# Routed attention and a gated FFN on one core: where the fill pieces of a unit begin, and a few one-hots, casts and copies put elsewhere

## The chip, the cores and the metric

The kernel runs on one core of a Trainium2 chip. A core has TensorE (matmuls, called PE in the profile), VectorE (DVE), ScalarE (ACT), GpSimd (POOL) and SyncE (SP), which work side by side, each through its own list of instructions in order, and wait for each other by semaphores. The metric is the device time of the program in microseconds, as the median of several executions. The profile is of one execution, and its span runs from the first to the last instruction, so it is a little shorter than the metric.

## The reference

First attention for 4 batches of 8 heads, 768 tokens and a head size of 64. Each query and each key is assigned to one of 16 clusters of its head, and a query sees only the keys of its own cluster. Then RMS norm and a gated FFN over 3072 tokens.

```python
q_assign = argmax(q_n @ c_n)          # 16 centroids for each head
k_assign = argmax(k_n @ c_n)
mask = q_assign[:, :, :, None] == k_assign[:, :, None, :]
scores = where(mask, scale * q @ k.T, -1e9)
attn = softmax(scores)
x = (attn @ v) as [3072, 512]
xn = x / sqrt(mean(x * x) + 1e-6) * rms_g
out = (silu(xn @ w_gate) * (xn @ w_val)) @ w_out      # 512 -> 1536 -> 512
```

## The kernel before

The work is cut into 8 units: four batches, two halves of the queries each. A unit has 8 heads, and a head 3 steps, each of which makes the scores of two blocks of 128 keys against 384 queries and one exponential. What PE does between two such steps is called a gap, so a unit has 24 gaps. The mask is in the matmul itself: below the 64 rows of a head's keys and queries lie 16 rows of one-hots of the cluster, so that an equal cluster adds a large number, which the bias of the exponential takes away again.

In PSUM there are two score tiles, one accumulator for a pair of heads (the pair is divided out of it before the next pair may use it), and three general tiles, which transposes, cluster products, gates, values and outputs share.

```python
ps_s = pool("ps_s", 2, space=PSUM)
ps_a = pool("ps_a", 1, space=PSUM)
ps_g = pool("ps_g", 3, space=PSUM)
```

A head goes through these helpers. `trans` turns tokens so that the head size lies on partitions, and has ACT or DVE copy the result out of PSUM. `cast` makes bf16 keys or queries of it (two halves each: K0, K1, Q0, Q1). `pair_clusters` finds the cluster of every token of two heads on PE and DVE. `under`, called by `head`, puts the one-hots below keys and queries with DVE transposes. `vcast` makes bf16 values on GpSimd. `pv` multiplies with the values and, at every second head, divides.

```python
def trans(g, h, part, on=None):
    ...                                     # 3 PE transposes into a ps_g tile
    if on is nc.vector:
        nc.vector.tensor_scalar_mul(to, ps, by)
    else:
        nc.scalar.activation(to, ps, ACT.Copy, scale=by)

def head(n):
    under(n, 1)                             # one DVE transpose for the keys
    under(n, 0)                             # and one for the queries

def pv(u, h):
    ...
    if h % 2 == 0:
        accs[u] = ps_a.tile([P, 2, HT, D + 1], F32, tag="acc", name="acc")
    ...                                     # 18 matmuls pT x vbf
    if h % 2:
        nc.vector.reciprocal(inv[:, :, :nt], acc[:, :, :nt, D])
        nc.vector.tensor_tensor(dst, acc[:, :, :nt, :D], ..., op=ALU.mult)
```

In unit 0 what goes into each gap is written out by hand. Gaps not named get `more`, one filler matmul on constants that keeps PE busy; gaps with `None` get nothing.

```python
early = [lambda h=h, m=m: trans(1, h, m, nc.vector if h > 2 else None) for h in (2, 3) for m in (1, 0)]
first = {0: lambda: trans(1, 0, 0), 1: gap1, 2: early[0], 3: early[1], 4: lambda: (early[2](), early[3]()), 5: gap5,
         6: None, 7: lambda: (head(4), head(5)), 9: lambda: pair_clusters(3), 10: None,
         13: lambda: (head(6), head(7)), 14: lambda: (more(), second_batch())}
```

From unit 1 on the gaps are filled with pieces of the FFN of the units before and with the preparation of heads to come. Each piece has a cost, and the rule spreads them evenly over the gaps. In units 2 to 7 the pieces are, in order: the last 8 gate and value products of unit u-2, the RMS norm of unit u-1, the output products of unit u-2 and the transposes of unit u-1, and then the gates and values of unit u-1 with the transposes, casts and clusters of the heads to come.

```python
def attention(heads, fill, skip=0, hooks={}):
    gaps = [(u, h, i) for u, h in heads for i in range(UNITS[u][2])]
    total, done, n = sum(c for c, _ in fill), 0.0, 0
    for at, (u, h, i) in enumerate(gaps):
        scores(u, h, i)
        if i == (0 if (u, h) == (1, 0) else 1):
            for p in due:
                pv(*p)                      # the head before this one
            due[:] = [(u, h)]
        ...
        while n < len(fill) and at >= skip and done <= total * (at + 1 - skip) / (len(gaps) - skip):
            done += fill[n][0]
            fill[n][1]()
            n += 1
```

Of the kernel before, what the change touches and what calls it, by code (L numbers as in the profile page):

```python
# [22 lines left out]
def kernel(  # L23
# [12 lines left out]
    nc = tc.nc  # L36
    B, H, S, D = q.shape
# [8 lines left out]
    NG = B * H // HG  # L46
    UNITS = [(b, c, HT) for b in range(B) for c in (0, HT)]
    NU = len(UNITS)
    CC = DM // P
# [4 lines left out]
    CUT = CC + 2 * FC - 8  # L54
# [30 lines left out]
    def load_qk(n):  # L85
        if n < B * H:
            load(n, 0)
            load(n, 1)
# [102 lines left out]
    def load_gv(i):  # L191
        c = slice(i * DF // 4, (i + 1) * DF // 4)
        for w, of in ((wg, moe_w_gate), (wv, moe_w_val)):
            nc.gpsimd.dma_start(out=w[:, :, c], in_=of[:, c].rearrange("(c p) f -> p c f", p=P))
# [7 lines left out]
    def trans(g, h, part, on=None):  # L202
        if (g, h // 2) not in qkT:
            qkT[g, h // 2] = qk32.tile([P, 2, 2, UQ], F32, tag="qkT", name="qkT")
        qk = staged[g * HG + h]
        ps = ps_g.tile([P, UQ], F32, tag="gen", name="tq")
        for i in range(HT):
            nc.tensor.transpose(ps[:, i * P:(i + 1) * P], qk[:, part, 2 * i:2 * i + 2].rearrange("p t d -> p (t d)"),  # L208
                                ident_f)
        to, by = qkT[g, h // 2][:, h % 2, part], 1.0 / ZS if part else 1.0  # L210
# [4 lines that stand above are left out]
# [5 lines left out]
    def cast(on, g, h, part, es=(0, 1)):  # L220
        for e in es:
            to = cols((kext if part else qext)[g % 4][:D, h], g, e)
            of = qkT[g, h // 2][e * D:(e + 1) * D, h % 2, part]
            if on is nc.scalar:
                nc.scalar.copy(to, of)
            else:
                on.tensor_copy(to, of)  # L227

    def vcast(n):
        nc.gpsimd.tensor_copy(vbf[n // HG % 4][:, n % HG, :, :D], stagedv[n])  # L230
# [62 lines left out]
    def slot(n, m):  # L293

        return 32 * (2 * (n % 2) + m if n < 2 else 2 * m + n % 2)

    def pair_clusters(p, heads=(0, 1)):
        g, h = divmod(2 * p, HG)
        what = [(h + i, m) for i in heads for m in range(2)]
        at = [slot(2 * p + i, m) for i in heads for m in range(2)]  # L300
        r = slice(min(at), max(at) + 32)
        pool = ps_g if p else ps_s
        ps = pool.tile([P, UQ], F32, tag="gen" if p else "s", name="sc")
        for a, (hh, m) in sorted(zip(at, what)):
            nc.tensor.matmul(ps[a:a + 32], lhsT=cblk[:, g * HG + hh], rhs=qkT[g, hh // 2][:, hh % 2, m],
                             start=True, stop=True)
        sct = asg.tile([P, UQ], F32, tag="scT", name="scT", bufs=2)
        nc.vector.transpose(sct[r], ps[r])
        cl = sct[r].rearrange("p (b e c) -> p b e c", e=2, c=NC)
        mx = small.tile([P, NB, 2], F32, tag="mx", name="mx")[r]  # L310
        nc.vector.tensor_reduce(mx, cl, axis=AX, op=ALU.max)
        nc.vector.tensor_tensor(pads[p][r, :, :NC].rearrange("p b c e -> p b e c"), cl,
                                mx.unsqueeze(3).broadcast_to([mx.shape[0], NB, 2, NC]), op=ALU.is_equal)

    def under(n, m):
        i = slot(n, m)
        nc.vector.transpose((kext if m else qext)[n // HG][D:D + 32, n % HG].bitcast(I32),
                            pads[n // 2][i:i + 32].rearrange("p b c e -> p (b c e)").bitcast(I32))
# [181 lines left out]
    def weave(t, c):  # L500

        return [x for pair in zip(t, c) for x in pair] + c[len(t):]

    def group(g):
        t, c, a = group_work(g)
        return [x for h in range(HG) for x in t[2 * h:2 * h + 2] + c[2 * h:2 * h + 2]] + a

    def spread(a, b):

        if not a:  # L510
            return list(b)
        w, n = [], 0
        for i, x in enumerate(a):
            w.append(x)
            while n < len(b) * (i + 1) // len(a):
                w.append(b[n])
                n += 1
        return w
# [12 lines left out]
    def border(o, ffn):  # L531

        return o[:-2] + ffn[:2] + o[-2:-1] + ffn[2:4] + o[-1:]
# [6 lines left out]
    def head(n):  # L540
        under(n, 1)
        under(n, 0)

    def casts(on, n, *what):
        for m, e in what:
            cast(on, n // HG, n % HG, m, (e,))

    K0, K1, Q0, Q1 = (1, 0), (1, 1), (0, 0), (0, 1)
    pool_ = nc.gpsimd
# [32 lines left out]
    def more():  # L582
        busy(1, False)
# [3 lines left out]
    def second_batch():  # L587
        nc.sync.dma_start(out=hold, in_=invs[0].rearrange("p a t -> p (a t)"))
        for n in range(H + HG, H + NQ):
            load_qk(n)  # L590
        for n in range(H, H + NV):
            load_v(n)
# [13 lines left out]

    def gap5():
        pair_clusters(2)
        casts(pool_, 6, Q0, K0, K1)
        vcast(4)  # L610
        casts(pool_, 7, Q0)
        for n in (4, 5):
            casts(pool_, n, Q1)
        vcast(5)
        casts(pool_, 7, K0, K1)
        vcast(6)
        load_gv(2)
        vcast(7)
        for n in (6, 7):
            casts(pool_, n, Q1)  # L620
        load_gv(3)

    early = [lambda h=h, m=m: trans(1, h, m, nc.vector if h > 2 else None) for h in (2, 3) for m in (1, 0)]
    late = [lambda h=h, m=m: trans(2, h, m, nc.vector if h < 3 else None) for h in range(HG) for m in (1, 0)]
    first = {0: lambda: trans(1, 0, 0), 1: gap1, 2: early[0], 3: early[1], 4: lambda: (early[2](), early[3]()), 5: gap5,
             6: None, 7: lambda: (head(4), head(5)), 9: lambda: pair_clusters(3), 10: None,
             13: lambda: (head(6), head(7)), 14: lambda: (more(), second_batch())}
    first.update({16: None, 19: None, 22: None})
    first.update({i: f for i, f in zip((15, 17, 18, 20, 21, 23), late)})

# [3 lines left out]
# [7 lines that stand above are left out]
                    pv(*p)  # L641
                due[:] = [(u, h)]
            if h == H - 1:
                squares(u, i, False)
            if (u, h, i) in hooks:
                hooks[u, h, i]()
# [4 lines that stand above are left out]
        for _, f in fill[n:]:  # L651
            f()

    attention([(0, h) for h in range(H)], [], hooks={(0, *divmod(i, HT)): f for i in range(H * HT) for f in [first.get(i, more)] if f})
    for u in range(1, NU):
        ffn, o, g = ffn_work(u - 1), out_work(u - 2) if u > 1 else [], u + 2
        if u == 1:
            t, c, a = group_work(2)
            t3, c3, a3 = group_work(3)
            n = LEAD - 4  # L660
            o3 = [(0.0, lambda i=i: load_o(i)) for i in range(0, FC, 4)]
            w = weave(t3[n:], c3)
            prep = c + a + w[:6] + spread(w[6:], o3) + a3[:5]
            idle = const.tile([P, 1], BF16)

            def norm():
                rms(0)
                nc.gpsimd.tensor_copy(idle, xn[0][:, HT - 1, DM - 1:])
                for h in range(HG):
                    casts(pool_, H + h, K0, Q0, K1, Q1)  # L670

            hooks = {(1, 0, 0): late[6], (1, 0, 1): lambda: (late[7](), norm())}
            hooks.update({(1, *divmod(2 + i, HT)): t3[i][1] for i in range(n)})
            hooks[1, *divmod(LEAD - 1, HT)] = lambda: xtrans_all(0)
            fill = spread(ffn[CC:CUT], prep)
            attention([(1, h) for h in range(H)], fill, LEAD, hooks)
        else:
            fill = ffn_work(u - 2)[CUT:] + [(0.0, lambda u=u: rms(u - 1))]
            fill += border(spread(o[:3], [(0.0, f) for _, f in a3[5:]]) + o[3:], ffn) if u == 2 else border(o, ffn)
            attention([(u, h) for h in range(H)], fill + spread(ffn[CC:CUT], group(g) if g < NG else []), 1)  # L680
    rest = ffn_work(NU - 2)[CUT:]
    rest[0][1]()
    pv(NU - 1, H - 1)
# [38 lines left out]
```

## Time and profile before

| what | value |
|---|---|
| time, median of 3 | 346.6 us (346.44 to 346.74) |
| span of the profiled execution | 344.7 us |
| PE busy | 337.5 us (98%) |
| ACT busy | 259.0 us (75%) |
| DVE busy | 222.5 us (65%) |
| POOL busy | 113.2 us (33%) |
| TensorE clock granted | 1.000 |

How to read it: "busy" counts the time in which at least one instruction of the engine runs. Rows of the timeline give the start in us, the length in us of a run of like instructions, engine, line of the kernel and operation, what is written and read, and how many. Square brackets at the end give the idle time of the engine just before, and what ended it. L333 are score matmuls and L337 their exponentials, L351 the products with the values, L358 the divisions, L423 gates and values, L448 the output products, L208 transposes, L212 and L214 their copies by DVE and ACT, L227 casts, L230 casts of values, L317 one-hots, L305 and L241 cluster products, L376 the squares of the norm, and L117 filler.

### The profile page before, as it was taken

What the parts mean: (1) busy time and instruction counts of PE and PEld (TensorE: products, weight loads), DVE (VectorE), ACT (ScalarE), POOL (GpSimd) and SP (SyncE); (2) the same over time, 40 slices, a digit from 0 to 9 for tenths busy, and PEclk for the clock granted to TensorE, in tenths of its full rate; (3) what the DMA queues carried; (4) which work ended last, traced back from release to release, by engine and by line L of the source; (5) the groups of instructions that cost most, each with busy time, mean ns of one, the idle gap of its engine ahead of it and who ended that gap; (6) DMA issues with size and microseconds to landing.
All of it is one profiled execution on the core that took longest, in us unless ns stands there. A gap on an engine that the chain in (4) does not pass through costs nothing.

```text
span 344.7 us, 7997 instructions
## 1 busy us (share of the span) xinstructions
PE 337.5 (98%) x3044; PEld 208.4 (60%) x3044; DVE 222.5 (65%) x540; ACT 259.0 (75%) x447; POOL 113.2 (33%) x227
## 2 busy tenths in 40 slices
PE   8999999999999999999999999999999999999996
PEld 4546657555765567565675656755566656655654
DVE  6999797976578626785367745686356645675330
ACT  5889979856888768886797777888778877764322
POOL 6999696234336205180132702435000000000000
PEclk9999999999999999999999999999999999999999
DMA  7999979982450014400130010000100001001002
GB/s 269 360 226 210 240 170 231 159 271 89 143 164 17 27 62 152 139 22 35 61 94 2 23 62 32 2 8 18 63 32 0 2 33 61 2 1 64 30 2 91
DMA packets 27302, 31.62 MB, mean 92 GB/s; under 512 B 4480, under 2 KB 24320, under 8 KB 27264
## 3 DMA queue, kind: packets, MB, share of 16 engines
q1 hardware_dynamic: 18608, 25.02, 22.3%
q0 software_dynamic: 8368, 5.71, 10.3%
q8 instruction: 24, 0.39, 0.5%
q10 hardware_dynamic: 288, 0.39, 0.3%
q14 instruction: 14, 0.11, 0.1%
HBM read 28.35 MB, written 6.29 MB: 100 GB/s over the span
## 4 chain that ended last, share of the span: by engine, by line
PE 87%; ACT 5%; POOL 3%; DVE 2%; DMA 1%; issue 1%; ACTq 0%; POOLq 0%; DVEq 0%
PE gate L423 17%; PE o L448 17%; PE val L423 17%; PE s L333 16%; PE acc L351 9%; PE tq L208 4%; ACT pT L337 4%; PE sc L241 3%; PE tx L396 1%; POOL kext L227 1%; DMA qk<-in_q_dram 1%; PE warm L117 1%; POOL qext L227 1%; PE o L459 1%; ACT xn L376 1%
## 5 line engine op out<-in xcount | busy, mean ns | idle before, releaser
L337 ACT ACTIVATE pT<-s,off 128x768 bf16<-128x768 f32 x192 | 170.8, 904 | 34.7 <-PE s L333 33.6
L333 PE MATMUL s<-qext,kext 80*128 80x384 bf16 x384 | 94.2, 327 | 1.6 <-ACT pT L337 0.6
L432 DVE SCALAR_TENSOR_TENSOR th<-th,gate 128x384 f32<-128x384 f32 x84 | 46.4, 552 | 50.3 <-ACT th L431 50.1
L423 PE MATMUL gate<-xnT,wg 128*128 128x384 bf16 x384 | 78.5, 325 | 0.1
L423 PE MATMUL val<-xnT,wv 128*128 128x384 bf16 x384 | 78.1, 326 | 0.0
L448 PE MATMUL o<-wo,gvT 128*128 128x512 bf16 x276 | 67.6, 379 | 0.0
L227 POOL CAST qext<-qkT 64x384 bf16<-64x384 f32 x64 | 34.5, 546 | 75.0 <-ACT qkT L214 66.6
L333 PEld LDWEIGHTS <-kext 80*128 80x128 bf16 x384 | 36.6, 98 | 31.2 <-issue 7.5
L431 ACT ACTIVATE th<-gate 128x384 f32<-128x384 f32 x84 | 41.2, 491 | 13.9 <-PE gate L423 13.5
L423 PEld LDWEIGHTS <-wv 128*128 128x128 bf16 x384 | 36.1, 97 | 25.3 <-issue 3.4
L423 PEld LDWEIGHTS <-wg 128*128 128x128 bf16 x384 | 35.9, 97 | 24.6 <-issue 3.3
L436 DVE SCALAR_TENSOR_TENSOR gvT<-th,val 128x384 bf16<-128x384 f32 x84 | 46.2, 549 | 6.1 <-PE val L423 1.4
L351 PEld LDWEIGHTS <-pT 128*128 128x128 bf16 x1152 | 43.5, 97 | 10.6 <-DVE x L358 1.3
L351 PE MATMUL acc<-vbf,pT 128*128 128x65 bf16 x1152 | 45.7, 193 | 1.2 <-POOL vbf L230 0.7
L448 PEld LDWEIGHTS <-gvT 128*128 128x128 bf16 x276 | 25.7, 97 | 25.5 <-issue 0.6
L208 PE MATMUL tq<-ident_f,qk 128*128 128x128 f32 x192 | 30.7, 279 | 0.0
L282 POOL DMA_DIRECT2D qext<-oh x40 | 19.1, 486 | 30.2 <-DVE oh L271 24.2
L397 DVE TENSOR_SCALAR xnT<-tx,gcol 128x384 bf16<-128x384 bf16 x28 | 10.6, 413 | 28.5 <-PE tx L396 28.5
L214 ACT ACTIVATE qkT<-tq 128x384 f32<-128x384 f32 x55 | 26.0, 494 | 3.6 <-PE tq L208 3.2
L208 PEld LDWEIGHTS tq<-ident_f,qk 128*128 128x128 f32 x192 | 23.8, 143 | 6.6 <-ACT qkT L214 1.0
L451 ACT COPY o_sb<-o 128x512 f32<-128x512 f32 x23 | 13.5, 586 | 17.7 <-PE o L448 17.7
L282 POOL DMA_DIRECT2D kext<-oh x40 | 19.1, 485 | 10.1 <-DVE oh L271 10.1
(81 smaller groups left out, 250.3 us busy)
## 6 DMA issues: line engine op xcount, KB each, us to landing
qk<-in_q_dram SPq DMA_DIRECT2D x32, 192.0 KB, 4.3
vs<-in_v_dram SPq DMA_DIRECT2D x32, 192.0 KB, 4.3
out_dram<-o_sb SPq DMA_DIRECT2D x23, 256.0 KB, 2.0
qk<-in_k_dram SPq DMA_DIRECT2D x30, 192.0 KB, 4.3
wg<-in_moe_w_gate_dram POOLq DMA_DIRECT2D x4, 384.0 KB, 8.1
wv<-in_moe_w_val_dram POOLq DMA_DIRECT2D x4, 384.0 KB, 10.5
wo<-in_moe_w_out_dram POOLq DMA_DIRECT2D x3, 512.0 KB, 8.8
qext<-oh POOLq DMA_DIRECT2D x40, 12.0 KB, 1.6
```

Of the source, the lines that this page charges most:

```text
L208: nc.tensor.transpose(ps[:, i * P:(i + 1) * P], qk[:, part, 2 * i:2 * i + 2].rearrange("p t d -> p (t d)"), ident_f)
L214: nc.scalar.activation(to, ps, ACT.Copy, scale=by)
L227: on.tensor_copy(to, of)
L282: on.dma_start(out=ext[D:D + NC, h, e * UQ:(e + 1) * UQ], in_=put[g, m][32 * h + e * NC:32 * h + (e + 1) * NC])
L333: nc.tensor.matmul(ps[:, j, :w] if nt == HT else flat[:, j * w:(j + 1) * w], lhsT=cols(kext[g % 4][:KR, hh], g, kc // HT, kc % HT * P, (kc ...
L337: nc.scalar.activation(pT[u, h][:, n * i:n * i + n, :w], of, ACT.Exp, bias=off, scale=scale * ZS)
L351: nc.tensor.matmul(acc[:, h % 2, t], lhsT=pT[u, h][:, kc, t * P:(t + 1) * P], rhs=vbf[g % 4][:, hh, kc % HT * 2 + kc // HT], start=kc == 0 ...
L423: nc.tensor.matmul(ps, lhsT=w[:, c, f * P:(f + 1) * P], rhs=xnT[u][:, c, :n], start=c == 0, stop=c == CC - 1)
L431: nc.scalar.activation(th, ps, ACT.Tanh, scale=0.5)
L432: nc.vector.scalar_tensor_tensor(th, th, 1.0, ps, op0=ALU.add, op1=ALU.mult)
L436: nc.vector.scalar_tensor_tensor(gvT[u][:, f, :n], gates[u], 0.5, ps, op0=ALU.mult, op1=ALU.mult)
L448: nc.tensor.matmul(outs[u], lhsT=gvT[u][:, f, t * P:(t + 1) * P], rhs=wo[:, f], start=f == 0, stop=f == FC - 1)
```

## The change

Its title is that a unit's pieces begin at its first gap instead of its second: `attention` gets no `skip` of 1 any more in units 2 to 7, so that pieces are placed from gap 0 on, and spread over 24 gaps rather than 23. It does so from a kernel that lacks some of what the one before has, so these go back at the same time:

- head 7's transposes are copied out of PSUM by ACT instead of DVE;
- head 6's keys are cast by DVE in gap 13 instead of by GpSimd in gap 5;
- the one-hots of head 4 are made in gap 5 instead of gap 7, and those of head 6 in gap 10 instead of gap 13, which puts them ahead of the divisions on DVE's list;
- gap 6 of unit 0 gets a filler matmul;
- the three loads of output weights are spread over all of the preparation of unit 1 but its first part, instead of starting six pieces later.

```diff
     def gap5():
         pair_clusters(2)
-        casts(pool_, 6, Q0, K0, K1)
+        casts(pool_, 6, Q0)
         vcast(4)
 ...
         load_gv(3)
+        head(4)
 
-    early = [lambda h=h, m=m: trans(1, h, m, nc.vector if h > 2 else None) for h in (2, 3) for m in (1, 0)]
+    early = [lambda h=h, m=m: trans(1, h, m) for h in (2, 3) for m in (1, 0)]
 ...
-             6: None, 7: lambda: (head(4), head(5)), 9: lambda: pair_clusters(3), 10: None,
-             13: lambda: (head(6), head(7)), 14: lambda: (more(), second_batch())}
+             7: lambda: head(5), 9: lambda: pair_clusters(3), 10: lambda: head(6),
+             13: lambda: (casts(nc.vector, 6, K0, K1), head(7)), 14: lambda: (more(), second_batch())}
 ...
-            w = weave(t3[n:], c3)
-            prep = c + a + w[:6] + spread(w[6:], o3) + a3[:5]
+            prep = c + a + spread(weave(t3[n:], c3), o3) + a3[:5]
 ...
-            attention([(u, h) for h in range(H)], fill + spread(ffn[CC:CUT], group(g) if g < NG else []), 1)
+            attention([(u, h) for h in range(H)], fill + spread(ffn[CC:CUT], group(g) if g < NG else []))
```

## Prediction

> **What bounds the kernel now.** I read the page first (busy time, then the chain that ended last), then a table of busy time by stage, then the instructions of TensorE and ScalarE in order of time in two places: the first unit (11 to 36 us) and the six places where one unit follows another. The page:
>
> ```profile
> PE 337.5 (98%) x3044; PEld 208.4 (60%) x3044; DVE 222.5 (65%) x540; ACT 259.0 (75%) x447; POOL 113.2 (33%) x227
> PE 87%; ACT 5%; POOL 3%; DVE 2%; DMA 1%; issue 1%; ACTq 0%; POOLq 0%; DVEq 0%
> ```
>
> TensorE (PE) is busy for 98% of the span, and 87% of the chain of waits is its work. The 98% is flattered, since the ends of matmuls are modelled and overlap the next start; so I count from start to start. In units 1 to 7 the stage table leaves it no idle time that could be seen:
>
> ```profile
> 41.00:107.36 66.36, 66.35 (x632) 40.98 (x631) 49.25 (x119) 52.61 (x85) 31.87 (x64) 1.00 0.66 168
> 107.36:148.40 41.04, 41.04 (x379) 25.69 (x377) 26.17 (x65) 32.78 (x60) 13.68 (x29) 1.00 0.26 83
> 267.40:304.20 36.80, 36.60 (x338) 22.74 (x338) 20.48 (x49) 29.67 (x53) 0.00 (x0) 1.00 0.06 23
> ```
>
> The columns are stretch, length, then busy time and count of PE, weight loads, DVE, ACT and POOL, then clock, DMA share and GB/s. Unit 3 (107.36 to 148.40) has 41.04 us of PE in 41.04, and ACT only 32.78. So from 41 us on the kernel is bound by TensorE, and only lost TensorE time can be won. Before that, in unit 0, ACT sets the pace. Its exponentials run in unbroken rows, and what stands in brackets is the little it waits:
>
> ```profile
> 16.30 1.72 ACT L337 ACTIVATE pT<-s,off 128x768 bf16<-128x768 f32 x2
> 18.35 3.28 ACT L337 ACTIVATE pT<-s,off 128x768 bf16<-128x768 f32 x4 [0.33 <-PE s L333]
> 21.86 0.90 ACT L337 ACTIVATE pT<-s,off 128x768 bf16<-128x768 f32 x1 [0.24 <-PE s L333]
> 23.10 4.92 ACT L337 ACTIVATE pT<-s,off 128x768 bf16<-128x768 f32 x6 [0.34 <-PE s L333]
> 28.70 1.69 ACT L337 ACTIVATE pT<-s,off 128x768 bf16<-128x768 f32 x2 [0.68 <-PE s L333]
> ```
>
> Six exponentials take 4.92 us in a row, 0.82 each. (A gap is one third of a head: two score matmuls and one exponential. Head h has gaps 3h to 3h+2.)
>
> **What the Trainium skill says.** "Perfetto Trace Analysis", section "Tensor Engine Instruction (MATMUL, LD_WEIGHTS)", says that the profiled end of a matmul is estimated, not observed, and that ACT, DVE and GpSimd take their work strictly in order. The trace agrees on the first: a gate piece of four matmuls is shown 0.81 us long, and the next begins 0.65 us after it. The second is what makes the order of emission in unit 0 matter; the DVE records of this trace stand in the order of the program. The same page, section "Identifying the Most-Contended Engine", warns that matmul busy time says little about closeness to the roofline; I use it only to find who waits. "ScalarE: Activation LUTs", section "What ACT_TABLE_LOAD costs", says that back-to-back activations overlap by about 93 ns; here one exponential is 904 ns on the page and 820 in a row, which agrees. "GPSIMD Engine Reference", section "Elementwise — side-by-side cycle accounting", has VectorE about twice as fast elementwise; here a 64x384 cast has a median of 504 ns on POOL and of 354 on DVE, so a factor of 1.4.
>
> **Part 1: pieces from the first gap (the title of the change).** With skip 1, the first gap of units 2 to 7 holds only its two score matmuls, so two pairs of scores follow each other at once, and then the product of the previous unit's last head. Two matmuls of a pair start 0.33 us apart from the next work (265.87 to 266.20), so four need 0.65. The trace at the borders from unit 1 to 2, from 2 to 3, and from 6 to 7:
>
> ```profile
> 65.33 0.98 PE L333 MATMUL s<-qext,kext 80*128 80x384 bf16 x4
> 66.16 0.53 PE L351 MATMUL acc<-vbf,pT 128*128 128x65 bf16 x12
> ```
>
> ```profile
> 107.36 0.89 PE L333 MATMUL s<-qext,kext 80*128 80x384 bf16 x4
> 108.08 0.28 PE L351 MATMUL acc<-vbf,pT 128*128 128x65 bf16 x4
> ```
>
> ```profile
> 266.85 0.49 PE L333 MATMUL s<-qext,kext 80*128 80x384 bf16 x2
> 267.60 0.48 PE L333 MATMUL s<-qext,kext 80*128 80x384 bf16 x2 [0.27 <-ACT pT L337]
> 267.93 0.71 PE L351 MATMUL acc<-vbf,pT 128*128 128x65 bf16 x18
> ```
>
> From the first score to the product it is 0.83, 0.72 and 1.08 us where 0.65 would do: 0.18, 0.07 and 0.43 lost. The second pair needs the score buffer of the last exponential of the old unit (there are two buffers), and that is not done; from unit 6 to 7 it is worst because ACT also makes squares there. The borders 3 to 4, 4 to 5 and 5 to 6 look like 2 to 3 (148.39 to 149.12, 189.44 to 190.16, 230.48 to 231.20): 0.07 each. Sum: 0.18 + 4 x 0.07 + 0.43 = 0.89 us.
>
> Working the fill rule through by hand (a piece is placed while the cost placed so far is no more than the share of the gaps passed), skip 0 puts two pieces, a gate and a value product, into gap 0 of every unit from 2 on. They are 1.3 us of PE between the two pairs of scores, more than the 0.43. So the waits go. In the last gaps of a unit the rule places the same pieces as before, so the load on ACT there stays. The RMS norm still comes behind the product of head 7 (gap 4 instead of 5), and the transposes that need it about five gaps later. No piece is added. This part: **-0.9 us**, less whatever of the wait reappears; I count -0.75.
>
> **Part 2: head 7's two copies go from DVE to ACT (gap 4, unit 0).** DVE loses the two at 18.23, 1.02 us together. ACT gains two, about 0.40 each in a row (three took 1.26 us at 9.40): 0.8 us between the exponentials of gaps 4 and 5. ACT stood idle for 0.33 before gap 6, and its exponential of gap 5 ended at 18.02, so gap 6 starts at about 18.02 + 0.8 - 0.1 = 18.7 rather than 18.35. **+0.3 us**, carried by the full score buffers to gap 10 (22.2 instead of 21.86).
>
> **Part 3: one-hots of heads 4 and 6 ahead of the divisions.** One-hots are two DVE transposes, 2 x 0.60 us. DVE without the two copies reaches the clusters of the third pair at 18.2 instead of 19.17, ends them at about 20.2, then makes head 4's one-hots (1.2) and only then the division, which ends at about 22.15 instead of 21.95. These are the rows before:
>
> ```profile
> 21.39 0.56 DVE L358 TENSOR_TENSOR x<-acc,inv 128x384 f32<-128x384 f32 x1
> 22.00 0.72 PE L351 MATMUL acc<-vbf,pT 128*128 128x65 bf16 x18 [0.18 <-DVE x L358]
> 26.66 0.56 DVE L358 TENSOR_TENSOR x<-acc,inv 128x384 f32<-128x384 f32 x1
> 27.61 0.71 PE L351 MATMUL acc<-vbf,pT 128*128 128x65 bf16 x18 [0.68 <-POOL vbf L230]
> ```
>
> The division frees the only accumulator. So head 2's product starts at 22.2 instead of 22.0, and gap 11's exponential at about 23.3 instead of 23.1: the 0.3 of part 2 becomes 0.2, not 0.5, because both waits stand side by side. The second division ends at about 27.4 instead of 27.2.
>
> **Part 4: head 6's key casts go from POOL to DVE.** POOL loses two casts in a row (1.44 us at 25.55), so the value cast at 27.05 comes at about 25.6. That cast is what head 4's product waited for until 27.61. Now the accumulator, free at about 27.4, is the last wait: gap 17's exponential at about 28.55 instead of 28.70. The casts cost DVE some 0.4 us each behind that division, so head 7's one-hots end near 29.4 (29.6 before). From 28.70 on ACT runs without a break to the end of the unit. Parts 2 to 4 together: **-0.15 us**.
>
> **Part 5: the rest.** One more filler matmul in gap 6, 0.2 us of PE that ACT hides. Head 5 and later heads still get their one-hots before their scores. The output weights are loaded earlier and spread wider in unit 1; PE shows no wait for them, so 0.
>
> Sum: 346.6 - 0.75 - 0.15 = **345.7 us**.
>
> **Rivals.** (a) ACT's extra 0.8 us stays on the path: unit 0 would end 0.3 to 0.8 us later, and with part 1 the time would be 346.2 to 346.7. For it: ACT is full from 28.70. Against it: the 0.68 us wait ahead of that absorbs it. (b) The waits at the borders only move: ACT does the same work, and a unit whose gaps hold less PE work (1.15 instead of 1.20 of the rule's cost in units with head preparation, 0.99 instead of 1.04 in unit 7) leaves it less time. Against it: the page has ACT 75% busy, and no other score in units 2 to 7 waits 0.2 us or more for it. The time would be 346.3. (c) Other phasing of pieces with the three general PSUM buffers: in unit 3 the value piece beside the cluster products starts 0.15 late (106.71, where 106.56 would do). If that shifts by 0.1 per unit, it is +-0.5 in all. (d) DVE becomes the bound of unit 0 (10.70 us busy of the 11.20 from 18.8 to 30): if the strided casts cost 0.7 each, head 7's one-hots slip to about 30, still ahead of its scores at 31.24. No loss.
>
> **Range and chances.** Part 1 lies between 0 and -0.9, parts 2 to 4 between -0.4 and +0.6, phasing adds +-0.4. That gives 345.0 to 346.6 at 8 in 10, with 345.7 in the middle. Two per cent are 6.9 us; nothing in the sum comes near it.
>
> **What would show it.** Right: at each border the two pairs of scores stand 1.0 us or more apart with gate and value pieces between, and the row waiting 0.27 us for ACT is gone; the PE idle of 267.4 to 304.2 drops; unit lengths from 107 to 230 go from 41.04 to just under 41.0. In unit 0, ACT's idle before gap 6 is gone, head 4's product waits for a division instead of a cast, and the row of exponentials that began at 28.70 begins at 28.4 to 28.7. Wrong, if unit 0 ends later than 28.70 + 8 exponentials (35.2) by more than 0.5 us, or if new PE waits appear within units 2 to 7.

## The result and the profile after

The changed kernel takes **348.28 us** (median of 4, 347.92 to 348.38), the kernel before 346.67 beside it: a ratio of 1.0046, 95% interval 1.0028 to 1.0063. It is 1.6 us slower where 0.9 us less was forecast. The page of the changed kernel, its busy times and its chain:

```profile
PE 338.8 (98%) x3045; PEld 208.4 (60%) x3045; DVE 221.3 (64%) x540; ACT 261.1 (75%) x449; POOL 112.8 (33%) x225
PE 85%; DVE 8%; ACT 5%; issue 1%; POOL 0%; ACTq 0%; DVEq 0%; POOLq 0%
```

The busy times hardly differ. The chain does: DVE holds 8% of it where it held 2%, and GpSimd, with 3% before, is gone. A share of the chain is not a loss, and part of this one lies in unit 0 (the page's list of the chain by line has L312 and L317 there with 1% each). But L432 and L436, which empty gates and values, and the key casts of L227 are in it too, with 1% each. That points to places where PE waits for DVE, which a page with PE busy for 98% in both kernels doesn't show.

The first question is whether the two gains that were forecast came at all. ScalarE in unit 0, in order of time:

```profile
17.94 4.12 ACT L337 ACTIVATE pT<-s,off 128x768 bf16<-128x768 f32 x5
22.28 0.90 ACT L337 ACTIVATE pT<-s,off 128x768 bf16<-128x768 f32 x1 [0.22 <-PE s L333]
23.46 4.91 ACT L337 ACTIVATE pT<-s,off 128x768 bf16<-128x768 f32 x6 [0.28 <-PE s L333]
28.55 6.45 ACT L337 ACTIVATE pT<-s,off 128x768 bf16<-128x768 f32 x8 [0.17 <-PE s L333]
```

The idle 0.33 us ahead of gap 6 is gone, filled by the two copies. Gap 10 comes at 22.28 instead of 21.86, and gap 17 at 28.55 instead of 28.70, its wait down from 0.68 to 0.17. Unit 0 is as forecast.

The border from unit 2 to unit 3, TensorE in order of time:

```profile
107.83 0.49 PE L333 MATMUL s<-qext,kext 80*128 80x384 bf16 x2
108.15 0.81 PE L423 MATMUL gate<-xnT,wg 128*128 128x384 bf16 x4
108.80 0.81 PE L423 MATMUL val<-xnT,wv 128*128 128x384 bf16 x4
109.45 0.49 PE L333 MATMUL s<-qext,kext 80*128 80x384 bf16 x2
109.78 0.40 PE L351 MATMUL acc<-vbf,pT 128*128 128x65 bf16 x8
```

Each piece starts when the one before has done: 0.32, 0.65, 0.65, 0.33. Nothing waits. From unit 6 to 7 it is the same (scores at 269.08 and 270.71, product at 271.04, a gate and a value between). So the gain at the borders came too, less 0.12 us that a value behind the first border now loses (70.07, due at 69.95).

The loss lies inside units 2 to 5. A unit, from one cluster product to the same in the next unit, takes 41.65 us (184.50 to 226.15) where it took 41.04 (182.81 to 223.85).

In unit 3 two places stand out where a matmul starts later than the ones before it need. TensorE and DVE there, all engines in order of time, some rows left out:

```profile
131.44 0.81 PE L423 MATMUL val<-xnT,wv 128*128 128x384 bf16 x4
...
132.41 0.90 PE L208 MATMUL tq<-ident_f,qk 128*128 128x128 f32 x6
132.74 0.35 DVE L227 CAST kext<-qkT 64x384 bf16<-64x384 f32 x1
133.13 0.55 DVE L436 SCALAR_TENSOR_TENSOR gvT<-th,val 128x384 bf16<-128x384 f32 x1
133.15 0.49 PE L333 MATMUL s<-qext,kext 80*128 80x384 bf16 x2
...
133.74 0.81 PE L423 MATMUL gate<-xnT,wg 128*128 128x384 bf16 x4
...
138.23 0.81 PE L423 MATMUL gate<-xnT,wg 128*128 128x384 bf16 x4
...
139.21 0.82 PE L208 MATMUL tq<-ident_f,qk 128*128 128x128 f32 x6
...
139.65 0.55 DVE L432 SCALAR_TENSOR_TENSOR th<-th,gate 128x384 f32<-128x384 f32 x1
140.25 0.81 PE L423 MATMUL val<-xnT,wv 128*128 128x384 bf16 x4 [0.23 <-DVE th L432]
```

Scores from 133.15 are done at 133.48, but the gate starts at 133.74: 0.26 lost. Two transposes from 139.21 need 0.65, but the value starts at 140.25: 0.39 lost. In both places two transposes stand side by side. There are three general PSUM tiles. If the two transposes take two of them, the next gate or value takes the one that the third piece back had. At 133.74 that is the value of 131.44, emptied by the DVE row that ends at 133.68; at 140.25 it is the gate of 138.23, emptied by the DVE row that ends at 140.20. With the 0.09 that the second transpose of 132.41 loses, a unit loses 0.74.

In the first place the emptying is late. The value's matmuls are done at 132.09, but on DVE its row comes behind that of the gate before it and a key cast (132.74), so that 1.59 us pass until 133.68. TensorE has other work for only 1.39 of them, until 133.48.

The kernel before has the very same order of pieces. Only the scores and the product lie elsewhere among them: at the first place a pair of scores lies between the two transposes, at the second a pair of scores and a product lie behind them. Its TensorE at the second place, with the DVE row that empties the gate's tile:

```profile
137.87 0.81 PE L423 MATMUL gate<-xnT,wg 128*128 128x384 bf16 x4
...
138.52 0.82 PE L208 MATMUL tq<-ident_f,qk 128*128 128x128 f32 x6
...
139.18 0.49 PE L333 MATMUL s<-qext,kext 80*128 80x384 bf16 x2
...
139.45 0.56 DVE L432 SCALAR_TENSOR_TENSOR th<-th,gate 128x384 f32<-128x384 f32 x1 [0.52 <-ACT th L431]
139.51 0.71 PE L351 MATMUL acc<-vbf,pT 128*128 128x65 bf16 x18
...
140.05 0.81 PE L423 MATMUL val<-xnT,wv 128*128 128x384 bf16 x4
```

Between the gate's end (138.52) and the value lie 1.53 us of other PE work, in the changed kernel 0.98 (138.88 to 139.86). Tanh and the DVE operation that empties the gate's tile are done 1.32 us after the gate's end in the changed kernel (138.88 to 140.20), so 0.98 doesn't cover them. In the kernel before they are done 1.49 after it (140.01), and nothing waits.

But cover is not all that differs. Rows of the kernel before at the first place, three engines, others left out:

```profile
131.33 0.81 PE L423 MATMUL val<-xnT,wv 128*128 128x384 bf16 x4
...
132.51 0.49 ACT L214 ACTIVATE qkT<-tq 128x384 f32<-128x384 f32 x1
...
132.70 0.55 DVE L436 SCALAR_TENSOR_TENSOR gvT<-th,val 128x384 bf16<-128x384 f32 x1
...
133.06 0.81 PE L423 MATMUL gate<-xnT,wg 128*128 128x384 bf16 x4
```

The gate of 133.06 starts before the value of 131.33 has been emptied (133.25), so it can't have the value's tile. It starts, 0.09 late, just after the first transpose has been copied out (133.00). So the tiles are not handed out strictly in turn. Which one a piece gets is fixed in the program when it is built, and in the two built programs, at both places of units 2 to 5, the gate or value has the tile of the first transpose in the kernel before, and that of the third piece back in the changed one.

### The profile page after: what moved, and what is told of

Same layout as the page of the kernel before. It is cut to its first block, busy times and chain, and to the rows that moved or that the text cites. A ratio compares the mean times of both kernels' runs of the same rounds, so it can differ in the third digit from the quotient of the medians.

```text
span 346.5 us, 8001 instructions
## 1 busy us (share of the span) xinstructions
PE 338.8 (98%) x3045; PEld 208.4 (60%) x3045; DVE 221.3 (64%) x540; ACT 261.1 (75%) x449; POOL 112.8 (33%) x225
## 4 chain that ended last, share of the span: by engine, by line
PE 85%; DVE 8%; ACT 5%; issue 1%; POOL 0%; ACTq 0%; DVEq 0%; POOLq 0%
PE o L448 17%; PE val L423 17%; PE gate L423 17%; PE s L333 15%; PE acc L351 9%; ACT pT L337 3%; PE tq L208 3%; PE sc L241 3%; DVE th L432 1%; PE tx L396 1%; DVE gvT L436 1%; DVE kext L227 1%; PE warm L117 1%; DVE pads L312 1%; DVE kext L317 1%
## 5 line engine op out<-in xcount | busy, mean ns | idle before, releaser
L432 DVE SCALAR_TENSOR_TENSOR th<-th,gate 128x384 f32<-128x384 f32 x84 | 46.1, 549 | 44.3 <-ACT th L431 42.8
L227 POOL CAST qext<-qkT 64x384 bf16<-64x384 f32 x64 | 35.2, 557 | 78.6 <-ACT qkT L214 71.0
L436 DVE SCALAR_TENSOR_TENSOR gvT<-th,val 128x384 bf16<-128x384 f32 x84 | 46.2, 550 | 11.0 <-PE val L423 6.5
L423 PEld LDWEIGHTS <-wv 128*128 128x128 bf16 x384 | 36.5, 97 | 27.4 <-issue 5.4
```

What stands on the lines that cost most here:

```text
L423: nc.tensor.matmul(ps, lhsT=w[:, c, f * P:(f + 1) * P], rhs=xnT[u][:, c, :n], start=c == 0, stop=c == CC - 1)
L432: nc.vector.scalar_tensor_tensor(th, th, 1.0, ps, op0=ALU.add, op1=ALU.mult)
L436: nc.vector.scalar_tensor_tensor(gvT[u][:, f, :n], gates[u], 0.5, ps, op0=ALU.mult, op1=ALU.mult)
```

## The experiments

The theory to test (T): the pieces themselves cost nothing new, but on other gaps two transposes come side by side without enough PE work around them, and a gate or value waits for a tile. Rivals: the parts put back in units 0 and 1 cost the time; a filled first gap costs as such; DVE's casts make the wait.

**Only the pieces, in the kernel before.**

```diff
-attention(..., fill + spread(ffn[CC:CUT], group(g) if g < NG else []), 1)
+attention(..., fill + spread(ffn[CC:CUT], group(g) if g < NG else []))
```

> Only part 1: the kernel before, with pieces from the first gap in units 2 to 7. Theory T (new phase): the pieces fall on other gaps, two transposes come side by side in units 2 to 5, and the next gate or value must wait for one of the three general PSUM tiles; +0.66 us in each of four units, less the 0.89 us won at the borders of units: about +1.75 us, 348.4. Rival R (the parts that were put back, in units 0 and 1, cost the time): 345.8, as predicted for part 1.

Measured: 348.84 us, ratio 1.0065 (1.0041 to 1.0089), and units of 41.65 us again. The title of the change alone makes all of the loss.

**Only the rest, in the changed kernel.** The same line, the other way round.

> Only parts 2 to 5: the changed kernel, with pieces from the second gap as before. Theory T: unit 0 ends 0.15 us earlier and nothing else changes, about 346.5. Rival R: 348 or more.

Measured: 346.41 us, ratio 0.9994 (0.9985 to 1.0004). The parts in units 0 and 1 together can't be told from nothing, and their forecast of 0.15 us less lies within that interval.

**Two pieces ahead, the others where they were**, in the kernel before.

```diff
...
-while n < len(fill) and at >= skip and done <= total * (...):
+while n < len(fill) and (at >= skip or n < lead) and (n < lead or done <= total * (...)):
...
-attention(..., 1)
+attention(..., 1, lead=2)
```

> The kernel before, with the two pieces of gap 1 of units 2 to 7 put into gap 0 and all other pieces left in the gaps where they were. Theory T: the border waits (0.89 us) go and no new ones come: 345.8. If the border waits only move elsewhere, it stays at 346.6; if it is a filled first gap as such that costs time, it is about 348.

Measured: 345.70 us, ratio 0.9971 (0.9960 to 0.9981). The border gain of 0.9 us is real; it had only been hidden under the new waits.

**From the first gap in units 6 and 7 alone.**

```diff
-attention(..., 1)
+attention(..., 1 if u < 6 else 0)
```

> The kernel before, with pieces from the first gap in units 6 and 7 alone, which prepare no heads and so have no transposes of tokens. Theory T: only border waits go (0.07 and 0.43 us) and no new ones come: 346.1. If the new phase costs in any unit, also without transposes, it is 346.6 to 347.3.

Measured: 346.03 us, ratio 0.9984 (0.9975 to 0.9993). Where no heads are prepared, new gaps do no harm.

**Transposes kept apart**, in the changed kernel.

```diff
-[x for h in range(HG) for x in t[2 * h:2 * h + 2] + c[2 * h:2 * h + 2]] + a
+[x for h in range(HG) for x in [t[2 * h]] + c[2 * h - 1:2 * h] + [t[2 * h + 1], c[2 * h]]] + c[-1:] + a
```

> The changed kernel, with the pieces of a head's preparation in another order (transpose of queries, last key cast of the head before, transpose of keys, first casts), so that a gate or value piece always lies between two transposes; no work is added or left out. If transposes side by side are what makes PE wait for a general PSUM tile, the waits of 0.09, 0.26 and 0.40 us in units 2 to 5 go: 348.28 - 3.0, about 345.3, at most 345.8. If it is only that the pieces lie in other gaps, it stays near 348.3.

Measured: 345.35 us, ratio 0.9963 (0.9950 to 0.9975); a unit takes 40.92 us. But the edit moves casts as well as transposes, so two further runs were made.

**The casts moved, the two transposes of a head next to each other in its list**, in the changed kernel.

```diff
+[x for h in range(HG) for x in t[2 * h:2 * h + 2] + c[2 * h - 1:2 * h] + [c[2 * h]]] + c[-1:] + a
```

> The changed kernel with the key cast moved as in the run with transposes kept apart, but the two transposes of a head left next to each other. By the fill rule one head in units 2 to 5 then still has both transposes and a gate in one gap, with no product between, where two places had waits before. Theory (transposes side by side, then a gate or value at once): one wait of about 0.3 to 0.4 us in each of four units stays, 345.35 + 4 x 0.35 = 346.7. Rival (the order of the casts on DVE was what helped): 345.4.

Measured: 345.31 us, ratio 0.9956 (0.9943 to 0.9968), as the rival said. The expectation was wrong about where the piece lies: the trace has the two transposes at 134.85, right behind a product at 134.31, and 0.08 us is all that the gate behind them loses. Nor did the edit leave the other transposes alone: with the casts in other places of the list, gates and values fall between them (a value at 131.37, a transpose at 132.02, a gate at 132.68). With no uncovered pair left, this run says nothing against T, and nothing for it.

**Two pairs of pieces swapped**, in the changed kernel, all casts left where they are among the pieces. In the list of pieces 0.3 is the cost of a transpose and 0.64 that of a gate or value.

```diff
+for i in range(len(fill) - 3, 0, -1):
+    if [w for w, _ in fill[i:i + 3]] == [0.3, 0.3, 0.64]:
+        fill[i + 1], fill[i + 2] = fill[i + 2], fill[i + 1]
```

> The changed kernel with only this: at the two places of units 2 to 5 where two transposes stand next to each other with a gate or value behind them, the second transpose and that gate or value change places. All casts keep their places among the other pieces. Theory (two transposes side by side ahead of a gate or value use up the tiles that are free, and it waits for DVE to empty a third): both waits go, a unit takes about 40.9 us instead of 41.65, 345.3. Rival (the casts on DVE make the wait, wherever the transposes stand): 347.5 to 348.3.

Measured: 345.75 us, ratio 0.9978 (0.9969 to 0.9987). TensorE of this run at the second place:

```profile
138.35 0.49 PE L208 MATMUL tq<-ident_f,qk 128*128 128x128 f32 x3
138.68 0.81 PE L423 MATMUL val<-xnT,wv 128*128 128x384 bf16 x4
```

The value now starts 0.33 behind its transpose, at once. A unit takes 41.03 us, so 0.62 of the 0.74 is won back and the rest stays in steps of 0.02 to 0.05 beside transposes. The order of two pieces decides, with the casts where they were.

**A cast taken from DVE**, in the changed kernel.

```diff
-cast(nc.vector, g, h, 1, (1,))
+cast(nc.gpsimd if g > 3 else nc.vector, g, h, 1, (1,))
```

> The changed kernel, with the second half of each head's keys (from unit 2 on) cast by GpSimd instead of DVE, which takes a cast of 0.35 us from between a gate's and a value's DVE operation. If the wait of 0.26 us is for the value's DVE operation behind that cast, it goes, and the one of 0.40 us gets 0.1 shorter: about 4 x 0.36 less, 346.9. If the waits are for ACT alone, nothing changes: 348.3.

Measured: 348.47 us, ratio 1.0052 (1.0038 to 1.0066): no gain. In its trace the wait of 0.26 is gone, and others have come in its place:

```profile
136.23 0.81 PE L423 MATMUL gate<-xnT,wg 128*128 128x384 bf16 x4
...
137.03 0.55 PE L208 MATMUL tq<-ident_f,qk 128*128 128x128 f32 x3
```

The gate that lost 0.26 follows its scores at once (133.62 behind 133.29). But the gate of 136.23 comes 0.10 late, and the transpose at 137.03, due at 136.88, 0.15 late. The cast was the last thing that the gate waited for, but taking it away only moved the wait to the next pieces of the same stretch.

**The product in the first gap of a head, and in its third**, in the changed kernel.

```diff
-if i == (0 if (u, h) == (1, 0) else 1):
+if i == (0 if (u, h) == (1, 0) or (u > 1 and h > 0) else 1):      # first
+if i == (0 if (u, h) == (1, 0) else 2 if u > 1 and h > 0 else 1):  # third
```

> The changed kernel with all pieces where they are, but the product with the values of the head before done in the first gap of a head instead of its second (units 2 to 7, heads 1 to 7). Its 0.55 us of PE then lie between the two transposes and the gate or value that waits, in both places. Theory (the tile's turn-around of some 1.3 us is not covered by 0.98 us of PE work): both waits go, 345.3, plus at most 0.3 for products that wait for their exponential. Rival (side by side alone counts, whatever lies between): 348.3.

> The same with the product in the third gap. It then lies before the first of the two waiting places, and nothing lies in the second (transposes and value in a first gap). Theory: the waits of 0.09 and 0.26 us go and that of 0.40 stays: 348.28 - 4 x 0.35, about 346.9. Rival: 348.3.

Measured: 347.40 us, ratio 1.0015 (1.0002 to 1.0029), for the first; 348.46, ratio 1.0046 (1.0033 to 1.0058), for the third. In the first, both named waits go: the gate follows its product at once, and the value behind the two transposes is 0.04 late instead of 0.39. But a new one has come at the pair of transposes (TensorE):

```profile
132.49 1.09 PE L208 MATMUL tq<-ident_f,qk 128*128 128x128 f32 x6
133.43 0.49 PE L333 MATMUL s<-qext,kext 80*128 80x384 bf16 x2
```

They need 0.65 and take 0.94, since the weight load of the second waits 0.29 for DVE to empty a gate's tile. A unit takes 41.35. In the third, the wait of 0.40 stays as expected, that of 0.26 shrinks to 0.11, and 0.17 appears at a later gate. The rule about cover held for the two places: in the first run the value behind the two transposes has the gate's tile too, which is emptied as late as in the changed kernel (1.32 us after the gate's end, 139.02 to 140.34), but now 1.53 us of PE work lie between. The sums were wrong, because moving the product uncovers other places. The second run also meets its rival's 348.3, so it doesn't decide.

**The best version.** The changed kernel with two pieces ahead, and that with the transposes kept apart as well:

> The changed kernel's unit 0 and loads, with two pieces in gap 0 of units 2 to 7 and the others in the gaps where they were in the kernel before. The gain at the borders and that of unit 0 should add: 345.7 - 0.15 = 345.55.

Measured: 345.57 us, ratio 0.9967 (0.9955 to 0.9980).

> The same as the run with two pieces ahead in the changed kernel, with the transposes kept apart as well. What is left of waits beside transposes there is 0.08 us in each of four units: 345.2 if they go, 345.6 if they don't matter.

Measured: **345.23 us**, ratio 0.9957 (0.9944 to 0.9969), units of 40.89 us. It beats both kernels. The run before it (345.57) and the changed kernel with only an order changed (345.35, 345.31) can't be told from it.

## Why the prediction was wrong

- **Part 1, the borders: right.** The 0.89 us of waits at six borders are gone in the trace, and moving two pieces alone won 0.9 us. The reason given for the longest of them, squares on ACT, doesn't set it apart: ACT makes squares at the border from unit 5 to 6 as well (230.72 in the trace before), where 0.07 us were lost.
- **Part 1, "the waits go" and nothing else: wrong.** The step that failed is that new gaps cost nothing inside the unit. The working looked at the first gap and the last ones, which do hold what it said; the new waits lie in between (gaps 15 and 18). This loss was named as rival (c), phasing with the three general PSUM tiles, and sized at 0.1 us per unit, taken from the one wait of 0.15 that the trace before has beside cluster products. It measured about 0.68 per unit in units 2 to 5 (41.65 - 41.04, and the 0.07 of a border that was won there), 2.7 us in four units. The new gaps could be worked out beforehand, and the time that a tile needs to come free stood in the trace before; the two were not held against each other. Which tile each piece would get could not be read from the trace before. The prediction's last sign of being wrong, new PE waits within units 2 to 7, is the one that came.
- **Parts 2 to 5: right in their steps; their sum of -0.15 is too small for the runs to confirm.** Gap 6, 10 and 17 were forecast at 18.7, 22.2 and 28.55, and came at 18.76, 22.28 and 28.55, though the whole trace starts its exponentials 0.13 later (11.15 instead of 11.02). The second division ended at 27.39 (27.4). Only the strided casts of head 6's keys were mis-sized: 1.08 us for two instead of 0.8, which ACT hid.
- **Rival (b), ACT short of time:** not seen; the three waits of scores for ACT that the changed kernel's trace has (0.28, 0.21 and 0.34 us) all lie before 41 us.
- **The sum:** -0.15 in unit 0 (not clear of noise), -0.89 at the borders, +2.7 within units give +1.7; measured +1.6.
- **The range** of 345.0 to 346.6 was too narrow by its phasing term: 0.4 us in all, against the 2.7 that four units with the same two waits add up to.

The Trainium skill, "Perfetto Trace Analysis", section "Optimization Strategy", says that the same gap repeating on the engine that should be saturated can mean too little SBUF or PSUM for the next tile. The trace agrees: 0.25 to 0.26 and 0.39 to 0.41 us, in each of four units. The experiments add that these waits go without a fourth tile when the order of the pieces is right; those beside the cluster products (0.09, 0.09 and 0.15 us in a unit, in both kernels) stay. A fourth tile wasn't tried. That a piece waited for its tile is read from the DVE row that ends 0.05 or 0.06 us before it starts; that part is inferred. Shown is that the pieces' new gaps make the loss, at two pairs of transposes, and that swapping two pieces there takes nearly all of it away. How much of it comes from the PE work that now lies elsewhere, and how much from the other tile that the same piece gets, no run separates.

## What to carry to other kernels

When an engine is full and its work is laid out by a rule, a new phase of the rule is a change of every wait, not only of those it was made for: list the pieces in their new order, see which tile each is given, and hold, for each, the PE work between the filling of that tile and its next use against the time that its emptying takes (here 0.98 us against 1.32, and 1.39 against 1.59). Two short pieces side by side (a transpose has 0.33 us of PE work, a gate 0.65) use up two tiles with little work to cover the emptying of the third. And a wait that is removed by speeding up its last releaser may return at the next piece, as it did here; changing the order took it away.

## What was not expected of the hardware

A cast of 64x384 from f32 to bf16 on DVE took 0.35 us where it writes consecutive elements (132.74), and two that write every second element took 1.08 us, with DVE not idle between them. Moving one of the first kind for each head, from unit 2 on, to GpSimd, which took 0.50 to 0.51 us for it, changed the time of the kernel by nothing that could be measured (the ratios to the kernel before, 1.0052 and 1.0046, lie in each other's intervals).
